# Four edits to a fused attention and mixture-of-experts kernel: opening order, half-size steps for the first pairs, a later request for the second batch, one engine for the last tile

## The chip, the core and the metric

The kernel runs on one core of a Trainium2 chip. The metric is the device time of one execution in microseconds, as the median of three runs. TensorE (PE) does matrix products into PSUM, VectorE (DVE), ScalarE (ACT) and GpSimd (POOL) do the elementwise work, SyncE (SP) issues nearly all DMA transfers, and 16 DMA engines carry them.

## What is computed

```python
scores = np.matmul(z, z.transpose(0, 2, 1)) / S      # 8 batches, S = 3072, z: 64 wide
attn = np.maximum(scores, 0.0) ** 2
x = (u * np.matmul(attn, v)).reshape(B * S, 256)     # u, v: 256 wide
# then a mixture of 8 experts over the rows of x, capacity 768 rows each, top 1:
# row -> expert by argmax(x @ w_gate); rows past the capacity give 0
out[i] = gate[i] * (np.maximum(x[i] @ w1[e], 0) @ w2[e])
```

Experts fill up in the order of the rows. So only the first 14 blocks of 512 rows are computed on the straight path (two batches of six blocks and two blocks of a third), and a guarded loop covers other data.

## The kernel before, in words

**Blocks and pairs.** A block is 512 rows of the output. It sums over 12 pairs; a pair is two tiles of 128 rows of v. For a pair that is made, PE computes scores (`team`, L924), ACT does relu twice and a square (L941, L946), DVE splits the square into a high and a low half-precision part (`hi` L950, `lo` L959), and PE adds up `acc` with three products per tile and 128 rows (L1070): 24 products of 128x256 a pair, half of a run of 48 that the trace shows as 5.41 us. The pairs of a block are p = 0 to 11 for the first, 12 to 23 for the second, 24 to 35 for the third, and so on; the blocks are counted from 0 in the code, block 1 being the second.

**What is not made again.** The scores are symmetric. A block writes the parts that later blocks need to `kept` in memory (`keep`, L981) and later blocks read them back transposed into `ld` (`load`, L897; asked for four pairs ahead, L1039). The part for the very next block goes straight to `nx` (L974), and a corner of the block on the diagonal is turned in the same way (L965). Block 1 writes six of these halves of 512 KB, block 2 four, block 3 two. Block 2 reads the pairs 24 and 25 back, block 3 the pairs 36, 37, 40 and 41, block 4 six pairs, block 5 eight.

**Scaling.** v is split into two half-precision parts too. For this the largest magnitude of a whole batch of v must be known: six parts of 512 KB are loaded (`ld_v`, L363), each reduced by ACT or DVE (`v_abs`, L484 and L73), then `v_red` (L492), a maximum over the partitions on POOL, and three DVE steps (`v_bits`) that make a power of two from it. Only then `v_piece` can split v (ACT L506, DVE L509). z is treated alike (`norm1` to `z_group`); in the first batch its first 12 tiles are turned by PE, the rest by DMA from a second load (`z_again`).

**What sets the order.** Every engine works through its own queue in order. The order is written when the kernel is built: a planner (`weave`, `Chain`) keeps a model clock of each engine and emits the next stage of a chain where it fits. The opening, up to the third pair, is instead written out by hand in `to_scores` and `to_sums`: `go(c, n)` emits the next n steps of a chain, `warm_up(n)` emits n products that nobody reads, which fill PE's queue. A batch that isn't the first is prepared by chains of low rank: a load waits until the model's DMA clock is close to now, and the squares and maxima follow some 20 us later.

**Where the second batch is asked for.** `hook(p)` calls `prepare` when a new block begins: for batch 1 at the start of block 1 (p = 12), for batch 2 at the start of the first block of batch 1. The last step of its z, a swap of halves, is held until pair p + 27.

**The last tile.** In `ffn` the rows of an expert's output are scaled from PSUM in two steps, ACT from one half of the accumulator (L1242) and DVE adding the other (L1248), and scattered by POOL (L84). For the very last tile both parts are summed on PE already, and ACT and DVE scale 128 columns each, into one tile `ys`.

Of the kernel before, what the change touches and what calls it, by code (L numbers as in the profile page):

```python
# [18 lines left out]
P = 128  # L19
# [7 lines left out]
def attention_moe_kernel(ctx: ExitStack, tc: tile.TileContext, u, v, z, w_gate, w1, w2, out, cap):  # L27
# [306 lines left out]
    def prepare(bt, first=False, swap=()):  # L334
# [140 lines left out]
        def v_abs(i):  # L475

            act = first and i in (0, 2, 4, NV)
# [12 lines left out]
        def v_red():  # L490
            bt.vmx = sm.tile([P, 1], F32, tag="vmx", name="vmx")
            nc.vector.tensor_reduce(out=bt.vmx, in_=bt.vm[:, 0:NM], axis=AX.X, op=ALU.max)  # L492
# [5 lines left out]
        def v_bits():  # L498
            bt.vs, bt.vinv = pow2(bt.vma, 1, 14 if first else 12, "vs")
            bt.v2 = sb.tile([P, JT, 2, D], F16, tag="big", name="v2")  # L500

        def v_piece(t0, k):
# [4 lines left out]

            def lo():
# [4 lines left out]

            return [[("ACT", 0.19 + 0.21 * k, hi, None)], [("DVE", 0.06 + 0.285 * k, lo, key("v", t0 // 2) if t0 + k > t0 // 2 * 2 + 1 else None)]]

        def factor():
            q = sm.tile([P, 1], F32, tag="cb0", name="cb0")
            q2 = sm.tile([P, 1], F32, tag="cb1", name="cb1")
            bt.cb = sm.tile([P, 1], F32, tag="cb", name="cb")
# [12 lines left out]
        if first:  # L532
            tz = [(ld_z(i)(), op("SP", 0.75))[1] for i in range(zparts)]
# [50 lines left out]
        def to_scores():  # L584
# [8 lines left out]
            go(A[0])  # L593
            go(G[0], 3)
# [5 lines left out]
            go(A[1])  # L600

        def to_sums(follow, more):
# [4 lines left out]
            go(follow[0])  # L607
# [3 lines left out]
            go(G[2])  # L611
# [13 lines left out]
            for t, k in ((0, 1), (1, 1), (2, 2)):  # L625
# [9 lines left out]
            go(V[2])  # L635
            go(G[2])
# [4 lines left out]
            for i in range(2, JT // 2):  # L641
# [195 lines left out]
    def attention(blocks, hook):  # L837

        NP = len(blocks) * NPAIR
        prs, acc, xs, ut, sct, sq, corner = {}, {}, {}, {}, {}, {}, {}  # L840
# [89 lines left out]
        def follow(p, s, w, t):  # L930
# [29 lines left out]

            def turn(c):
# [17 lines left out]
            def keep():  # L979
# [7 lines left out]
                  [("DVE", 0.07 + w * 0.00107, hi, None, bt.key("vs")), ("DVE", 0.29 + w * 0.0021, lo, (aid, "a", p))]]  # L987
# [46 lines left out]
        for p in range(NP):  # L1034
# [11 lines left out]
            for c in range(cc):  # L1046
                if c % (cc // 2) == 0:
                    scores_to(p + 3 if p > 3 else p + 2 if p or c else 0)
                    weave()
                if c == 0:  # L1050
# [5 lines left out]
                if i == 0 and c % 2 == 0:  # L1056
# [8 lines left out]
                for jj in (0, 1):  # L1065
# [114 lines left out]
    def ffn(wx, sx, n, final):  # L1180
# [43 lines left out]
        for t in range(T):  # L1224
# [14 lines left out]
            def scale(t=t, y=y, end=end):  # L1239
# [4 lines left out]
            def add(t=t, y=y, end=end):  # L1244
                if end:
                    ts(ys[t][:, D // 2:], y[:, 0, D // 2:], g[:, t:t + 1], ALU.mult)
                else:
                    nc.vector.scalar_tensor_tensor(out=ys[t], in0=y[:, 1], scalar=g[:, t:t + 1], in1=ys[t],  # L1248
                                                   op0=ALU.mult, op1=ALU.add)

            Chain([[("ACT", 0.36, scale, None)], [("DVE", 0.4, add, (fid, "y", t))],
# [51 lines left out]
    with tc.manual_schedule():  # L1303
# [40 lines left out]
        def hook(p):  # L1344
# [4 lines left out]
            if g == 0 and ib == (b == 0) and b + 1 in bats:  # L1349
# [82 lines left out]
```

## Time and profile before

| | us |
|---|---|
| median of three runs (782.4 to 784.85) | 783.13 |
| the profiled execution | 783.24 |
| its span in the profile | 781.4 |

The profiled execution took 783.24 us, its span as the profile has it is 781.4 us. Times in a row of the timeline are counted from the start of the span; the first number is the start, the second the time until the last instruction of that row ended. "x2" is two instructions of a kind in a row, and a bracket tells how long the engine sat idle before, and what ended that. SPq is SyncE's queue, which issues DMAs.

### The profile page before, as it was taken

What the parts mean: (1) busy time and instruction counts of PE and PEld (TensorE: products, weight loads), DVE (VectorE), ACT (ScalarE), POOL (GpSimd) and SP (SyncE); (2) the same over time, 40 slices, a digit from 0 to 9 for tenths busy, and PEclk for the clock granted to TensorE, in tenths of its full rate; (3) what the DMA queues carried; (4) which work ended last, traced back from release to release, by engine and by line L of the source; (5) the groups of instructions that cost most, each with busy time, mean ns of one, the idle gap of its engine ahead of it and who ended that gap; (6) DMA issues with size and microseconds to landing.
All of it is one profiled execution on the core that took longest, in us unless ns stands there. A gap on an engine that the chain in (4) does not pass through costs nothing.

```text
span 781.4 us, 16289 instructions
## 1 busy us (share of the span) xinstructions
PE 770.1 (99%) x6476; PEld 569.9 (73%) x6476; DVE 515.4 (66%) x1134; ACT 401.2 (51%) x690; POOL 120.8 (15%) x122
## 2 busy tenths in 40 slices
PE   9999999999999999999999999999999999999996
PEld 3787878888887777878888877886666666656664
DVE  7996888853517789974553258989576575574651
ACT  6966545533206657663431048675455464463541
POOL 0000102020202010210202020202420321313302
PEclk9999999999999999999999999999999999999999
DMA  7659999999978949999979959960698955944001
GB/s 223 147 193 196 250 202 228 207 217 183 182 156 182 289 147 183 236 199 215 204 145 194 171 165 240 320 178 22 216 299 297 321 143 216 294 129 174 28 15 44
DMA packets 283830, 149.49 MB, mean 191 GB/s; under 512 B 229741, under 2 KB 255674, under 8 KB 283744
## 3 DMA queue, kind: packets, MB, share of 16 engines
q1 hardware_dynamic: 278848, 135.57, 71.8%
q0 software_dynamic: 4896, 12.79, 4.7%
q8 instruction: 52, 0.85, 0.5%
q14 instruction: 34, 0.28, 0.1%
HBM read 36.25 MB, written 59.92 MB: 123 GB/s over the span
## 4 chain that ended last, share of the span: by engine, by line
PE 92%; DMA 2%; DVE 2%; SPq 1%; ACT 1%; issue 0%; POOL 0%; POOLq 0%; ACTq 0%
PE acc L1070 52%; PE hps L1211 15%; PE yps L1235 15%; PE sc L924 8%; DMA ld<-kept 1%; SPq L897 1%; DMA wraw<-in_moe_w 1%; PE lg L696 1%; PE warm L151 1%; DMA zraw<-in_z 1%; ACT a L946 0%; DVE wt L1138 0%; ACT r L941 0%; DVE hl L950 0%; DVE zz L425 0%
## 5 line engine op out<-in xcount | busy, mean ns | idle before, releaser
L1070 PE MATMUL acc<-v,hl 128*128 128x256 f16 x2280 | 261.0, 273 | 0.0
L1070 PEld LDWEIGHTS <-hl 128*128 128x128 f16 x2280 | 219.8, 98 | 34.2 <-issue 5.1
L941 ACT ACTIVATE r<-sc 128x512 f32<-128x512 f32 (+1 forms) x212 | 105.6, 550 | 166.2 <-PE sc L924 164.4
L1211 PE MATMUL hps<-fxt,wt 128*128 128x384 f16 (+2 forms) x816 | 127.4, 316 | 0.4 <-DVE hh L1197 0.3
L1235 PE MATMUL yps<-wt,hh 128*128 128x256 f16 (+1 forms) x776 | 126.6, 324 | 0.0
L959 DVE TENSOR_TENSOR hl<-a,hl 128x1024 f16<-128x1024 f32 (+1 forms) x106 | 118.2, 1115 | 3.6
L84 POOL DMA_INDIRECT disp<-xr,slot x54 | 60.8, 1126 | 378.3 <-ACT r L941 139.0
L1211 PEld LDWEIGHTS <-wt 128*128 128x128 f16 x816 | 77.6, 98 | 47.7 <-issue 0.9
L1235 PEld LDWEIGHTS <-hh 128*128 128x128 f16 x776 | 75.7, 98 | 48.5
L1070 PE MATMUL acc<-v,ld 128*128 128x256 f16 x960 | 109.2, 273 | 1.9 <-DMA ld<-kept 1.9
L946 ACT ACTIVATE a<-r 128x1024 f32<-128x1024 f32 (+1 forms) x106 | 102.6, 968 | 2.2
L1070 PEld LDWEIGHTS <-ld 128*128 128x128 f16 x960 | 93.0, 98 | 13.3 <-DMA ld<-kept 2.2
L950 DVE CAST hl<-a 128x1024 f16<-128x1024 f32 (+1 forms) x106 | 67.6, 638 | 49.9 <-ACT a L946 49.1
L1197 DVE SCALAR_TENSOR_TENSOR hh<-hps,hh 128x384 f16<-128x384 f32 (+2 forms) x136 | 70.6, 530 | 34.0 <-ACT hh L1196 33.6
L1196 ACT ACTIVATE hh<-hps 128x384 f16<-128x384 f32 (+2 forms) x136 | 63.7, 472 | 50.4 <-PE hps L1211 49.0
L84 POOL DMA_INDIRECT out<-ys,sid x48 | 53.4, 1112 | 128.4 <-DVE ys L1248 74.6
L924 PE MATMUL sc<-zz 64*128 64x512 f16 (+1 forms) x636 | 71.5, 356 | 0.3 <-DVE zz L425 0.2
L1242 ACT ACTIVATE ys<-yps,sg 128x256 f32<-128x256 f32 (+1 forms) x48 | 22.5, 471 | 72.6 <-PE yps L1235 68.2
L1070 PE MATMUL acc<-v,nx 128*128 128x256 f16 x504 | 58.5, 273 | 0.0
L1248 DVE SCALAR_TENSOR_TENSOR ys<-yps,sg,ys 128x256 f32<-128x256 f32 x47 | 22.6, 482 | 51.3 <-ACT ys L1242 50.8
L1070 PEld LDWEIGHTS <-nx 128*128 128x128 f16 x504 | 48.5, 98 | 8.3 <-issue 2.8
L678 ACT ACTIVATE xr<-x,rsr 128x256 f16<-128x256 f32 x54 | 24.8, 502 | 55.4 <-DVE rsr L60 51.8
(133 smaller groups left out, 484.2 us busy)
## 6 DMA issues: line engine op xcount, KB each, us to landing
out<-zero SPq DMA_DIRECT2D x48, 512.0 KB, 9.6
kept<-hl SPq DMA_DIRECT2D x40, 512.0 KB, 4.8
wraw<-in_moe_w SPq DMA_DIRECT2D x32, 512.0 KB, 6.4
vraw<-in_v SPq DMA_DIRECT2D x18, 512.0 KB, 6.4
u<-in_u SPq DMA_DIRECT2D x13, 512.0 KB, 5.1
zraw<-in_z SPq DMA_DIRECT2D x2, 768.0 KB, 6.3
zz<-zz SPq DMA_DIRECT2D x4, 384.0 KB, 4.5
xt<-xr SPq DMA_TRANSPOSE x54, 2.8
```

Of the source, the lines that this page charges most:

```text
L84: r = nc.gpsimd.indirect_dma_start(out=dst, out_offset=bass.IndirectOffsetOnAxis(ap=idx, axis=0), in_=src, in_offset=None, bounds_check=bo ...
L678: return lambda: nc.scalar.activation(st.x16[:, c, 0:D], st.x[:, c, :], AF.Copy, scale=st.rs[:, c:c + 1])
L924: nc.tensor.matmul(s[jj][:, 0:w], lhsT=bt.zz[rows, (kl + jj) % 2, j * P:(j + 1) * P], rhs=bt.zz[rows, (ql + jj) % 2, q0:q0 + w], start=(i ...
L941: nc.scalar.activation(sct[p][:, jj, :], s[jj][:, 0:w], AF.Relu)
L946: nc.scalar.activation(sq[p], sct.pop(p), AF.Square)
L950: nc.vector.tensor_copy(hl[:, :, :, 0, :], sq[p].rearrange("p j (t k) -> p j t k", k=HB))
L959: nc.vector.tensor_sub(hl[:, :, :, 1, :], a.rearrange("p j (t k) -> p j t k", k=HB), hl[:, :, :, 0, :])
L1070: nc.tensor.matmul(o, lhsT=a(h, jj, c), rhs=bt.v2[:, j, l], start=(i + jj + h + l + c % 2 == 0), stop=(i == NPAIR - 1 and jj + h == 2), sk ...
L1196: Chain([[("ACT", 0.05 + w * 0.00083, lambda: nc.scalar.activation(th, src, AF.Relu), None)], [("DVE", 0.07 + w * 0.00104, lambda: nc.vect ...
L1197: [("DVE", 0.07 + w * 0.00104, lambda: nc.vector.scalar_tensor_tensor(out=tl, in0=src, scalar=0.0, in1=th, op0=ALU.max, op1=ALU.subtract), ...
L1211: nc.tensor.matmul(o, lhsT=wx.w1[:, d, wp, f * P:(f + 1) * P], rhs=sx.xt[:, xp * DC + d, a:a + w], start=(q == 0), stop=(q == len(seq) - 1))
L1235: nc.tensor.matmul(y[:, 0 if end else l], lhsT=hid(i, f)[:, sl], rhs=w[:, l], start=(f + i == 0 and l != 1), stop=(f == FC - 1 and i == 1) ...
```

## The change

- Opening, loads: parts 0 and 1 of z are asked for in one DMA; v's part 0 is asked for from ACT's queue, behind a one-column Square that reads a cell which DVE fills with 2^-112 at the very beginning. That cell takes part in the maximum.
- Opening, order: v's part 1 is reduced by ACT, ahead of z's third group, instead of by DVE. z's `lo` of the third group and half of the first pair's `lo` come before v's maximum is known. `v_bits` makes the factor in two steps instead of three; the inverse moves to `factor`, which runs in the second half of the first block. The warm-up products after the first scores go from 20 to 13.
- First two pairs by tiles: `lo` in two halves of 128x512, v's piece for the second pair's `lo` in two of 128x256, and PE goes through the first tile for all four row groups, then through the second. v's piece for the third pair, and the third pair's `hi` and `lo`, get fixed places.
- The second batch's z and v are asked for at the start of block 2 instead of block 1 (p = 24), and the hold on the swap moves with p, to pair 51.
- The last tile is scaled by ACT alone, all 256 columns.

```diff
@@ prepare
-                    bt.vm = sm.tile([P, NV + 1], F32, tag="vm", name="vm")
+                    bt.vm = sm.tile([P, NV + 2], F32, tag="vm", name="vm")
+                    if first:
+                        nc.vector.memset(bt.vm[:, NM:NM + 1], 2.0 ** -112)
...
-                nc.sync.dma_start(out=zt[:, i * k:(i + 1) * k], in_=zr[:, i * k:(i + 1) * k])
+                o = slice(0, 2 * k) if first and i == 0 else slice(i * k, (i + 1) * k)
+                nc.sync.dma_start(out=zt[:, o], in_=zr[:, o])
...
-                nc.sync.dma_start(out=t, in_=vr[:, 4 * i:4 * i + 4, :])
+                if first and i == 0:
+                    one = sm.tile([P, 1], F32, tag="one", name="one")
+                    nc.scalar.activation(one, bt.vm[:, NM:NM + 1], AF.Square)
+                (nc.scalar if first and i == 0 else nc.sync).dma_start(out=t, in_=vr[:, 4 * i:4 * i + 4, :])
...
-            act = first and i in (0, 2, 4, NV)
+            act = first and i in (0, 1, 2, 4, NV)
...
-            bt.vs, bt.vinv = pow2(bt.vma, 1, 14 if first else 12, "vs")
+            if first:
...
+                ts(e, bt.vma.bitcast(I32), 23, ALU.logical_shift_right)
+                ts(rs, e, -float(1 << 23), ALU.mult, float(268 << 23), ALU.add)
+                bt.vs, bt.vinv = rs.bitcast(F32), inv.bitcast(F32)
+                bt.v_inv = lambda: ts(inv, rs, -1.0, ALU.mult, float(254 << 23), ALU.add)
+            else:
+                bt.vs, bt.vinv = pow2(bt.vma, 1, 12, "vs")
...
+            if first and t0 == 2:
+                return [[("ACT", 0.61, hi, None)], [("DVE", 0.38, lo_one(0), None), ("DVE", 0.38, lo_one(1), key("v", 1))]]
@@ to_scores
             go(A[0])
+            go(A[1])
             go(G[0], 3)
...
-            go(A[1])
@@ to_sums
             go(A[3])
-            go(follow[0])
+            go(G[2])
+            go(follow[0], 2)
             go(A[4])
             warm_up(2)
             third = more()[0]
-            go(G[2])
...
             go(vr, 3)
             go(follow[0])
-            warm_up(11)
+            warm_up(2)
             go(G[2])
-            warm_up(2)
+            warm_up(9)
             more()
-            warm_up(5)
...
             go(follow[1], 2)
             go(V[2])
+            go(follow[1])
+            go(V[2])
...
             go(third)
+            go(V[4])
+            go(third)
+            go(V[4])
+            go(third)
@@ attention, follow
-                  [("DVE", 0.07 + w * 0.00107, hi, None, bt.key("vs")), ("DVE", 0.29 + w * 0.0021, lo, (aid, "a", p))]]
+                  [("DVE", 0.07 + w * 0.00107, hi, None, bt.key("vs")), *([("DVE", 0.29 + w * 0.0021, lo, (aid, "a", p))] if p >= EARLY else
+                    [("DVE", 0.65, lo_half(0), None), ("DVE", 0.65, lo_half(1), (aid, "a", p))])]]
@@ attention, main loop
-            for c in range(cc):
+            for c, jjs in ([(c, (jj,)) for jj in (0, 1) for c in range(cc)] if p < EARLY else [(c, (0, 1)) for c in range(cc)]):
...
-                for jj in (0, 1):
+                for jj in jjs:
@@ ffn, the last tile
-                o = slice(0, D // 2 if end else D)
-                nc.scalar.activation(ys[t][:, o], y[:, 0, o], AF.Copy, scale=g[:, t:t + 1])
+                nc.scalar.activation(ys[t], y[:, 0], AF.Copy, scale=g[:, t:t + 1])
...
-                if end:
-                    ts(ys[t][:, D // 2:], y[:, 0, D // 2:], g[:, t:t + 1], ALU.mult)
@@ hook
-            if g == 0 and ib == (b == 0) and b + 1 in bats:
+            if g == 0 and ib == 2 * (b == 0) and b + 1 in bats:
                 prepare(bats[b + 1], swap=(("pair", p + 2 * NPAIR + 3),))
```

`EARLY` is 2 for the first batch and 0 otherwise.

## Rows read from the trace of the kernel before

**Rows 1.** The page: busy time, share of the span and instructions of each engine.
```profile
PE 770.1 (99%) x6476; PEld 569.9 (73%) x6476; DVE 515.4 (66%) x1134; ACT 401.2 (51%) x690; POOL 120.8 (15%) x122
```

**Rows 2.** Timeline of PE, 94 to 260 us: start, length, what; in brackets idle before.
```profile
102.18 2.79 PE L1070 MATMUL acc<-v,ld 128*128 128x256 f16 x24 [1.91 <-DMA ld<-kept]
...
137.24 5.40 PE L1070 MATMUL acc<-v,ld 128*128 128x256 f16 x48
```

**Rows 3.** Chain of waits, 70 to 106 us: start, length, what.
```profile
93.38 0.58 SPq L363
...
94.00 8.13 DMA ld<-kept
```

**Rows 4.** Windows: stretch, length, busy of each engine, PEclk, DMA share, GB/s.
```profile
80.00:100.00 20.00, 20.00 (x202) 16.39 (x199) 16.53 (x36) 9.12 (x14) 4.88 (x4) 1.00 1.09 254
...
120.00:140.00 20.00, 20.00 (x189) 16.36 (x188) 16.16 (x37) 9.94 (x15) 5.34 (x5) 1.00 1.08 266
```

**Rows 5.** Timeline of SP's queue, 50 to 260 us.
```profile
83.95 0.54 SPq L363 DMA_DIRECT2D vraw<-in_v  x1
...
125.69 8.51 SPq L897 DMA_TRANSPOSE ld<-kept  x2
```

**Rows 6.** DMA issues, 124 to 136 us: count, median us from issue to landing.
```profile
ld<-kept SPq DMA_TRANSPOSE x2, 6.6
```

**Rows 7.** Windows of the opening, columns as in Rows 4.
```profile
4.00:5.00 1.00, 1.00 (x5) 0.46 (x4) 0.54 (x1) 0.82 (x2) 0.00 (x0) 1.00 0.90 254
...
9.00:10.00 1.00, 0.99 (x10) 0.45 (x8) 0.97 (x4) 0.77 (x3) 0.00 (x0) 1.00 1.08 375
```

**Rows 8.** Timeline of the opening, up to the common factor of v.
```profile
3.80 0.63 ACT L370 ACTIVATE sq<-zraw 128x512 f32<-128x512 f32 x1 [1.77 <-DMA zraw<-in_z]
...
5.80 0.63 ACT L370 ACTIVATE sq<-zraw 128x512 f32<-128x512 f32 x1 [0.56 <-DMA zraw<-in_z]
...
8.22 1.06 ACT L484 ACTIVATE junk<-vraw 128x1024 f32<-128x1024 f32 x1 [1.79 <-DMA vraw<-in_v]
...
11.18 1.06 ACT L484 ACTIVATE junk<-vraw 128x1024 f32<-128x1024 f32 x1 [0.42 <-DMA vraw<-in_v]
...
12.19 2.32 DVE L73 TENSOR_REDUCE vm<-vraw 128x1 f32<-128x1024 f32 x2
...
15.81 0.63 ACT L484 ACTIVATE junk<-vraw 128x512 f32<-128x512 f32 x1 [0.38 <-DMA vraw<-in_v]
...
15.81 0.69 DVE L73 TENSOR_REDUCE vm<-vraw 128x1 f32<-128x512 f32 x1 [0.16 <-DMA vraw<-in_v]
...
17.64 0.15 DVE L60 TENSOR_SCALAR vsr<-vsi 128x1 int32<-128x1 int32 x1
```

**Rows 9.** Timeline of the opening, after the common factor of v.
```profile
17.71 1.22 DVE L959 TENSOR_TENSOR hl<-a,hl 128x1024 f16<-128x1024 f32 x1
...
18.64 1.04 ACT L946 ACTIVATE a<-r 128x1024 f32<-128x1024 f32 x1
...
18.84 0.87 DVE L509 SCALAR_TENSOR_TENSOR v<-vraw,vsr,v 128x256 f16<-128x256 f32 x2
...
21.58 0.75 DVE L509 SCALAR_TENSOR_TENSOR v<-vraw,vsr,v 128x512 f16<-128x512 f32 x1
...
25.18 1.22 DVE L959 TENSOR_TENSOR hl<-a,hl 128x1024 f16<-128x1024 f32 x1
...
26.39 5.41 PE L1070 MATMUL acc<-v,hl 128*128 128x256 f16 x48
```

**Rows 10.** Timeline, 36 to 60 us, a difference of half the usual width.
```profile
55.44 0.69 DVE L959 TENSOR_TENSOR hl<-a,hl 128x512 f16<-128x512 f32 x1
```

**Rows 11.** Timeline of the last tile and the one before it.
```profile
771.42 0.48 ACT L1242 ACTIVATE ys<-yps,sg 128x256 f32<-128x256 f32 x1 [2.13 <-PE yps L1235]
...
774.04 0.37 ACT L1242 ACTIVATE ys<-yps,sg 128x128 f32<-128x128 f32 x1 [2.14 <-PE yps L1235]
...
774.44 0.35 DVE L58 TENSOR_SCALAR ys<-yps,sg 128x128 f32<-128x128 f32 x1 [2.03 <-ACT ys L1242]
```

More of the change, by code (lines that the diff above doesn't have):

```diff
@@ L491, in v_red @@
             bt.vmx = sm.tile([P, 1], F32, tag="vmx", name="vmx")
-            nc.vector.tensor_reduce(out=bt.vmx, in_=bt.vm[:, 0:NM], axis=AX.X, op=ALU.max)
+            nc.vector.tensor_reduce(out=bt.vmx, in_=bt.vm[:, 0:NM + first], axis=AX.X, op=ALU.max)
         def v_all():
@@ L498, in v_bits @@
         def v_bits():
-            bt.vs, bt.vinv = pow2(bt.vma, 1, 14 if first else 12, "vs")
+            if first:
+                e = sm.tile([P, 1], I32, tag="vse", name="vse")
+                inv = sm.tile([P, 1], I32, tag="vsi", name="vsi")
+                rs = sm.tile([P, 1], I32, tag="vsr", name="vsr")
+                ts(e, bt.vma.bitcast(I32), 23, ALU.logical_shift_right)
[4 more added lines that the diff above has]
+                bt.vs, bt.vinv = pow2(bt.vma, 1, 12, "vs")
             bt.v2 = sb.tile([P, JT, 2, D], F16, tag="big", name="v2")
@@ L506, in hi, with lo_one, f @@
                 nc.scalar.activation(bt.v2[:, o, 0, :], bt.vraw[i][:, a:a + k], AF.Copy, scale=bt.vs)
+            def lo_one(j):
+                def f():
+                    nc.vector.scalar_tensor_tensor(out=bt.v2[:, t0 + j, 1, :], in0=bt.vraw[i][:, a + j], scalar=bt.vs,
+                                                   in1=bt.v2[:, t0 + j, 0, :], op0=ALU.mult, op1=ALU.subtract)
+                return f
             def lo():
@@ L518, in factor @@
             q2 = sm.tile([P, 1], F32, tag="cb1", name="cb1")
+            if first:
+                bt.v_inv()
             bt.cb = sm.tile([P, 1], F32, tag="cb", name="cb")
@@ L532, in prepare @@
         if first:
-            tz = [(ld_z(i)(), op("SP", 0.75))[1] for i in range(zparts)]
+            tz = [0.0] * zparts
+            for i in (0, 2):
+                ld_z(i)()
+                tz[i] = op("SP", 0.75 if i else 1.5)
+            tz[1] = tz[0]
             clk["DMA"] += 1.9
@@ L640, in to_sums @@
             go(third)
-            for i in range(2, JT // 2):
+            go(V[4])
+            go(third)
+            go(V[4])
+            go(third)
+            for i in range(3, JT // 2):
                 Chain(v_piece(2 * i, 2), -2, done[key("vs")], gate=("pair", i - 2 + (2 < i < 6)))
@@ L839, in attention @@
         NP = len(blocks) * NPAIR
+        EARLY = 2 if hasattr(blocks[0][0], "to_scores") else 0
         prs, acc, xs, ut, sct, sq, corner = {}, {}, {}, {}, {}, {}, {}
@@ L959, in lo, with lo_half, f @@
                 nc.vector.tensor_sub(hl[:, :, :, 1, :], a.rearrange("p j (t k) -> p j t k", k=HB), hl[:, :, :, 0, :])
+            def lo_half(j):
+                def f():
+                    a, hl = sq[p]
+                    nc.vector.tensor_sub(hl[:, j, :, 1, :], a[:, j].rearrange("p (t k) -> p t k", k=HB), hl[:, j, :, 0, :])
+                return f
             def turn(c):
@@ L1055, in attention @@
                     a = prs.pop(p)
-                if i == 0 and c % 2 == 0:
+                if i == 0 and c % 2 == 0 and 0 in jjs:
                     k = bank[0] - 3
@@ L1238, in ffn, with scale, add @@
                 weave()
-            def scale(t=t, y=y, end=end):
+            def scale(t=t, y=y):
                 ys[t] = sb.tile([P, D], F32, tag="hl", name="ys", bufs=5)
-                o = slice(0, D // 2 if end else D)
-                nc.scalar.activation(ys[t][:, o], y[:, 0, o], AF.Copy, scale=g[:, t:t + 1])
-            def add(t=t, y=y, end=end):
-                if end:
-                    ts(ys[t][:, D // 2:], y[:, 0, D // 2:], g[:, t:t + 1], ALU.mult)
[L1247 to L1251, printed above, removed]
+                nc.scalar.activation(ys[t], y[:, 0], AF.Copy, scale=g[:, t:t + 1])
+            def add(t=t, y=y):
+                nc.vector.scalar_tensor_tensor(out=ys[t], in0=y[:, 1], scalar=g[:, t:t + 1], in1=ys[t],
+                                               op0=ALU.mult, op1=ALU.add)
+            Chain([[("ACT", 0.36, scale, (fid, "y", t) if end else None)],
+                   [] if end else [("DVE", 0.4, add, (fid, "y", t))],
                    [("POOL", 1.04, lambda t=t: scatter("out", out, tid[:, t:t + 1], ys[t], NTOK - 1), None)]],
```

6 lines of the change are left out of this document (3 added, 3 removed).

## The prediction

> **What bounds the kernel now.** I read the page first: PE is busy for 770.1 us [rows 1], so out of the execution's 783.24 us only 13.1 are left that are not products, and a faster engine elsewhere is worth nothing unless it takes away PE idle time, or products that nobody reads. I then looked for PE's gaps, stage by stage. There are three places: the opening, where PE is kept busy with warm-up products until v is scaled; one gap in the middle; and the end, after the last product. The rest is products back to back, so what is gained in one place stays gained, unless a new gap opens behind it.
>
> The gap in the middle stands on PE's timeline: 1.91 us before the second read-back of block 2 (pair 25) [rows 2]. SP's queue and the chain of waits say why: one part of batch 1's v was issued at 83.95, ahead of the first read-back [rows 5], another at 93.38 between the two, and the second read-back took 8.13 us to land, at 102.13 [rows 3]. PE wanted it at 102.18 - 1.91 = 100.27. The windows show the DMA engines full there (share 1.09, 254 GB/s) [rows 4].
>
> For the opening I followed the timeline back from the first real products. Two places decide. The factor of v is ready at 17.64 + 0.15 = 17.79, and before it both engines wait for v's last part: ACT 0.38 us, DVE 0.16, both starting at 15.81 [rows 8]. Behind it DVE works without a gap until the low part of the third pair ends at 25.18 + 1.22 = 26.40, and PE begins that pair at 26.39 [rows 9]. Its third product is the first to read that low part; 48 products take 5.41 us, so it starts about 0.22 later, at 26.61. There are 0.2 us to spare, no more. An earlier first product alone therefore wins nothing: PE would wait at the third pair. What counts is when the factor is ready, and how long DVE's list behind it is.
>
> **The change, part by part.**
>
> *The later request.* Batch 1's z and six parts of v leave block 1. So the two parts of v no longer stand ahead of the late read-back; each is 0.52 MB, 2.1 us at 254 GB/s [rows 4], and two make 4.1. Without them it lands near 98.0, 2.3 us before PE wants it. So the gap closes: -1.91. The gain can't exceed the gap, and is 0 if something else of that stretch is as late.
>
> The same loads now lie in block 2, so the next thing to be late would be block 3's read-backs (pairs 36, 37). Before, the two were issued from 125.69 on, 8.51 us for both [rows 5], so the second at about 129.9; they land 6.6 us after issue [rows 6], the second at 136.5. (The row is a median of the two, so this is an estimate.) PE wants it half of its run after 137.24 [rows 2], at 139.9. That is 3.4 us of room, and the whole front moves alike. What comes in front of them, by the picture of block 1, is two parts of v: at 266 GB/s [rows 4] 2 x 1.97 = 3.9 us. What goes: block 2 writes two halves of 0.52 MB fewer than block 1, but that is in the 3.4 already; z's four transposes, which now fall in block 3, leave. So the sum is 3.4 - 3.9, about -0.5 at worst and some 2 of room at best. I take no new gap, and keep 0.5 for the range. ACT's and DVE's steps for batch 1 move along and have time until block 6; that cover goes only if their loads slip by blocks.
>
> *Loads of the opening.* DMA moved 254 GB/s between 4 and 5 us and 375 between 9 and 10 [rows 7]. If a second queue fills that hole, v's last part comes 1 x (375 - 254) / 375 = 0.3 us earlier. z in one DMA less frees SP's queue a step earlier, which is the same gain seen from SP. On ACT, the small Square and the issue stand ahead of the first square of z, where ACT waits 1.77 us for z anyway [rows 8]: no cost, unless issuing takes longer than that. The fill on DVE stands ahead of the constants, under the same wait for z. The inverse goes to DVE in the second half of block 0, one step of 0.15, and the swap held to pair 51 is wanted in block 6 only: nothing for both.
>
> Here the trace and a rule part. The trace has all these loads in one queue, and its rate between 4 and 5 us is a third below that of 9 to 10 [rows 7]. The Trainium skill, in "DMA: Bandwidth & Descriptors", section "Issuing engines are not separate DMA queues", says that DMAs of all issuers run on the same 16 engines and interleave, so that a second issuer saves only the time to issue. By that rule the 0.3 would be nothing; the second rival gives what the interleaving would do to z.
>
> *Order before the factor.* DVE loses one of the two maxima that took 2.32 us [rows 8] and gains half of the first pair's low part, 0.69 [rows 10]: 0.47 less. It was free 0.16 before 15.81 [rows 8], so it is free near 15.2, or 15.5 if z comes 0.3 later. ACT gets the maximum: 1.06. From v's first part at 8.22 to 15.43 ACT was waiting only for v's third part (0.42) and a little for PE [rows 8]. Its list from v's first part on is then 7.21 - 0.42 + 1.06 = 7.85. If that part still lands at 8.22 ACT reaches v's last part at 16.07, 0.26 late. Behind z it took 8.22 - 5.80 = 2.42 us [rows 8], where 0.52 MB at 375 GB/s [rows 7] take 1.4; from a queue of its own it may land up to 1.0 earlier, and I take 0.6, giving 15.5. So all three, the load, DVE and ACT, say 15.5 to within 0.3: the last maxima start 0.3 earlier than 15.81 (bounds: 0.26 later, 0.6 earlier). The factor then takes one DVE step less, 0.15 [rows 8]. Factor: 0.3 + 0.15 = 0.45 earlier, at 17.34.
>
> *Order behind the factor.* The first pair's low part is now 0.69 instead of 1.22 [rows 9, 10], but the saving is lost: the second pair's `hi` must wait for ACT's square, which ended at 18.64 + 1.04 = 19.68, and ACT's list from the factor to there is unchanged. Then come the halves: two of 0.69 for one of 1.22 (+0.16), and two pieces of one tile, which together took 0.87, for one of 0.75 (+0.12) [rows 9]. So the third pair's low part ends at 26.40 - 0.45 + 0.28 = 26.23. With the 0.2 to spare, PE starts the third pair 0.37 us earlier than before. The 7 warm-up products fewer keep PE out of the way; they are in this number, not beside it. Bounds: 0.2 us slower (factor 0.11 later, DVE's list 0.28 longer, 0.2 to spare) and 0.9 faster (last part 0.6 and step 0.15 earlier, the 0.2 to spare, with the cost of the halves hidden in DVE's waits for ACT).
>
> *The last tile.* DVE began its half only when ACT had ended, and ended at 774.44 + 0.35 = 774.79; ACT alone, at 0.48 for 256 columns, ends at 774.04 + 0.48 = 774.52 [rows 11]. The scatter starts on the one that is last: -0.27. Bounds: 0 and -0.35.
>
> *Sum.* -1.91 - 0.37 - 0.27 = -2.55, from 783.24 to 780.69. The median of the runs is 0.11 below that execution, so 780.6.
>
> **The rivals.**
>
> *The gap comes back a block later.* For it: block 2's DMA was as full as block 1's (1.08 and 1.09) [rows 4], and the room at pair 37 is about the size of what comes in. If three transfers of 1.97 stand in front of the read-back, it is 5.9 - 3.4 = 2.5 us late. 780.6 + 2.5 = 783.1: no difference. Against it: block 2 has two writes fewer, and the planner holds v back when its own DMA clock is busy.
>
> *The opening gives nothing, or less.* If v's first part takes half the engines while z's last third is under way (0.26 MB at 254 GB/s, 1.0 us), z lands up to 1.0 later than the 5.80 of before [rows 8]. DVE is then free for v's last part at 15.2 + 1.0 = 16.2, 0.4 late; less the step of 0.15, with the longer list (0.28) and less the 0.2 to spare that is 0.3 slower instead of 0.37 faster. 780.6 + 0.7 = 781.3: no difference that can be told, though the gap in the middle is gone. This is also the case in which the part of the change that gives its name to the opening doesn't do what it says. The rule of the Trainium skill named above is this rival's reason; in the opening of this trace only SP issues loads, so nothing shows it here.
>
> *Slower: block 3's read-backs stand behind all of v.* One mechanism: SP's queue is in order, and if the planner places all six parts of v before pair 37's read-back they cost 6 x 1.97 = 11.8 us of transfers, less 3.4 of room: PE stands 8.4 us. 780.6 + 8.4 = 789.0. It turns slower by over 0.3% from 5 us of standing on, which is more than four parts of v in front. Against it: in block 1 the parts were spread over the whole block, one of them was still issued between two read-backs [rows 3].
>
> **How the numbers follow.** 0.3% is 2.35 us, about what a measurement of this kernel can tell from no change; the border of faster is 780.78, close to my sum, so the forecast's own spread lies on both sides. Chances: the forecast 0.52, of which 0.45 below the border; the gap a block later 0.25; the opening giving nothing 0.13; slower 0.10. That makes faster 0.45, same 0.07 + 0.25 + 0.13 = 0.45, slower 0.10. Range: the low end is the forecast with the opening's best (0.5 more), the last tile's best (0.1) and half a microsecond of spread between runs, 779.5; the high end is the gap coming back, 783.1, with a little of that spread, 783.4. The slower case and half of the spread beyond the gap stay outside.
>
> **What would show it.** The gap before pair 25 gone from PE's idle time, and no read-back of pairs 36, 37, 40, 48 in front of a new one. The factor of v ready near 17.3, and PE's third pair starting near 26.0, with z's last square starting no later than 6.1. ACT alone on the last tile, the scatter 0.3 us sooner after the last product. I am wrong if PE's second block starts less than 0.2 us earlier, if ACT reaches v's last part later than it lands, or if a read-back in blocks 3 to 5 is waited for.

## The result and the profile after

The changed kernel took 787.34 us (median of 7 runs), beside 782.40 for the kernel before in the same comparison: a ratio of 1.0068, 95% interval 1.0048 to 1.0088. By the ratio it is 5.3 us slower, where 2.55 less were forecast, and it lies outside the range. The profiled execution took 789.47 us, its span 787.7.

PE's line of the page (columns as in [rows 1]) shows where to look. PE is busy for 771.6 us, 1.5 more than before although it makes seven products fewer, and idle for 787.7 - 771.6 = 16.1 us, 4.8 more than before. DVE and ACT did about the same work as before, so the loss is not in their busy sums.

```profile
PE 771.6 (98%) x6469; PEld 569.7 (72%) x6469; DVE 514.1 (65%) x1136; ACT 401.8 (51%) x693; POOL 121.8 (15%) x122
```

PE's timeline of the changed kernel, blocks 2 to 5 (start, length, what; idle before in brackets), shows where it stood:

```profile
100.02 5.40 PE L1112 MATMUL acc<-v,ld 128*128 128x256 f16 x48
...
137.69 5.40 PE L1112 MATMUL acc<-v,ld 128*128 128x256 f16 x48
...
155.59 2.25 PE L1112 MATMUL acc<-v,hl 128*128 128x256 f16 x19 [0.29 <-DVE hl L994]
...
177.01 4.09 PE L1112 MATMUL acc<-v,ld 128*128 128x256 f16 x36 [1.21 <-DVE x L1054]
...
211.79 5.42 PE L1112 MATMUL acc<-v,ld 128*128 128x256 f16 x48 [1.27 <-DMA ld<-kept]
...
232.38 5.42 PE L1112 MATMUL acc<-v,ld 128*128 128x256 f16 x48 [1.68 <-DMA ld<-kept]
```

The first two rows are the places that the prediction watched. The gap of 1.91 us before pair 25 is gone: pairs 24 and 25 now run their 48 products without a break, and so do pairs 36 and 37, as they did before [rows 2]. But four gaps are new, 0.29 + 1.21 + 1.27 + 1.68 = 4.45 us, and the first two of them end on DVE, not on a DMA.

The other loss is in the opening. Its timeline in the changed kernel, and the last of these rows as the kernel before has it:

```profile
0.74 1.28 ACT L368 ACT_TABLE_LOAD   x1 [0.74 <-PEq L1459]
0.91 0.42 ACTq L369 DMA_DIRECT2D vraw<-in_v  x1
...
2.04 0.20 ACT L368 ACTIVATE one<-vm 128x1 f32<-128x1 f32 x1
7.05 1.67 ACT L376 ACTIVATE sq<-zraw 128x512 f32<-128x512 f32 x3 [4.81 <-DMA zraw<-in_z]
...
11.80 0.62 PE L425 MATMUL ztp<-ident,zhl 128*128 128x128 f16 x8 [1.56 <-DVE zhl L414]
13.45 2.93 PE L959 MATMUL sc<-zz 64*128 64x512 f16 x12
...
20.12 0.15 DVE L60 TENSOR_SCALAR vsr<-vse 128x1 int32<-128x1 int32 x1
...
28.65 5.68 PE L1112 MATMUL acc<-v,hl 128*128 128x256 f16 x48
34.26 1.47 PE L959 MATMUL sc<-zz 64*128 64x512 f16 x12
```

```profile
31.73 1.47 PE L924 MATMUL sc<-zz 64*128 64x512 f16 x12
```

The second row is the surprise. The code puts the one-column Square (2.04) in front of the issue of v's part 0, but the issue went out at 0.91, during the table load: it depends on nothing that the Square writes. z's squares then begin at 7.05, where they ran at 3.80 and 5.80 before [rows 8]; PE gets z 1.56 us too late, the factor of v ends at 20.27 instead of 17.79, and the third pair starts at 28.65 instead of 26.39 [rows 9]. The scores after it begin at 34.26 instead of 31.73, 2.53 later.

The windows of the same stretch (columns as in [rows 4]), and the first of them in the kernel before:

```profile
3.00:4.00 1.00, 1.00 (x3) 0.30 (x2) 0.48 (x3) 0.00 (x0) 0.00 (x0) 1.00 0.90 176
4.00:5.00 1.00, 1.00 (x4) 0.40 (x3) 0.00 (x0) 0.00 (x0) 0.00 (x0) 1.00 1.10 371
...
14.00:16.00 2.00, 2.00 (x12) 0.57 (x6) 2.00 (x4) 1.25 (x4) 0.00 (x0) 0.50 1.28 245
```

```profile
3.00:4.00 1.00, 1.00 (x3) 0.29 (x2) 0.45 (x3) 0.20 (x1) 0.00 (x0) 1.00 1.04 301
```

Between 4 and 5 us the DMA engines moved 371 GB/s instead of 254 [rows 7], but between 3 and 4 only 176 instead of 301, so over the two they moved no more than before (547 for 555). The hole was not filled, it moved, and part of what came were bytes of v that nobody could use yet, while ACT and DVE did nothing at all between 4 and 5. The last row of the changed kernel shows a granted clock of 0.50, the 1.2 GHz level: 12 products for scores take 2.93 us there and 1.47 at 34.26, and the difference is about what PE is busy longer than before.

The last tile came out as forecast. The changed kernel's timeline, and the scatter of the kernel before:

```profile
780.04 0.47 ACT L1283 ACTIVATE ys<-yps,sg 128x256 f32<-128x256 f32 x1 [2.15 <-PE yps L1277]
780.79 0.97 POOL L84 DMA_INDIRECT out<-ys,sid  x1 [1.13 <-ACT ys L1283]
```

```profile
775.07 0.97 POOL L84 DMA_INDIRECT out<-ys,sid  x1 [1.41 <-DVE ys L58]
```

The scatter starts 0.75 after ACT does; before it was 1.03 (ACT's start is in [rows 11]). That is 0.28 less, where 0.27 was forecast.

Summed up: 2.53 (opening) + 4.45 (new gaps) - 1.91 (old gap) - 0.28 (last tile) = 4.8. The two profiled executions are 6.2 apart and the medians 5.3 or so by the ratio. The rest is spread over three places, as the same rows of the two profiles show. The changed kernel is 2.53 late behind the opening, 0.45 at the sum of block 2 (136.58 for 136.13) and 5.57 at that of block 5 (247.20 for 241.63), which is 0.5 more than the gaps alone explain; it is still 5.57 late at the last block (528.08 for 522.51). The mixture adds 0.43 (last tile 780.04 for 774.04). And from the start of the last scatter to the end of the span it is 6.9 us instead of 6.3; that tail is 5.5 to 6.9 in all the profiles of this case, old kernel or new.

### The profile page after: what moved, and what is told of

Its sections match the earlier page's. It is cut to its first block, busy times and chain, and to the rows that moved or that the text cites. A ratio compares the mean times of both kernels' runs of the same rounds, so it can differ in the third digit from the quotient of the medians.

```text
span 787.7 us, 16284 instructions
## 1 busy us (share of the span) xinstructions
PE 771.6 (98%) x6469; PEld 569.7 (72%) x6469; DVE 514.1 (65%) x1136; ACT 401.8 (51%) x693; POOL 121.8 (15%) x122
## 4 chain that ended last, share of the span: by engine, by line
PE 81%; issue 7%; DMA 4%; DVE 4%; ACT 1%; POOL 1%; SPq 1%; POOLq 0%; ACTq 0%
PE acc L1112 46%; PE hps L1253 13%; PE yps L1277 13%; PE sc L959 8%; DMA ld<-kept 2%; DMA fxt<-disp 2%; POOL out L84 1%; DMA zraw<-in_z 1%; DVE v L530 1%; SPq L723 1%; PE lg L730 1%; DVE hl L985 0%; SPq L932 0%; DVE hl L994 0%; DVE wt L1180 0%
## 5 line engine op out<-in xcount | busy, mean ns | idle before, releaser
L994 DVE TENSOR_TENSOR hl<-a,hl 128x1024 f16<-128x1024 f32 (+1 forms) x104 | 115.7, 1113 | 3.5
L1283 ACT ACTIVATE ys<-yps,sg 128x256 f32<-128x256 f32 x48 | 22.6, 472 | 72.6 <-PE yps L1277 68.2
```

Of the source, the lines that this page charges most:

```text
L994: nc.vector.tensor_sub(hl[:, :, :, 1, :], a.rearrange("p j (t k) -> p j t k", k=HB), hl[:, :, :, 0, :])
```

## Where the new gaps come from

The views of SP's queue, ACT and DVE in block 3 of the changed kernel, in order of time:

```profile
126.00 9.19 SPq L932 DMA_TRANSPOSE ld<-kept  x2
...
136.43 3.73 SPq L1006 DMA_TRANSPOSE corner<-hl  x2
140.25 4.22 SPq L932 DMA_TRANSPOSE ld<-kept  x2
144.56 3.07 SPq L466 DMA_TRANSPOSE zz<-zhl  x2
...
149.02 0.61 ACT L459 ACTIVATE zhl<-zraw,zb 128x384 f16<-128x384 f32 x1 [6.33 <-DMA zz<-zhl]
...
149.67 0.62 DVE L462 SCALAR_TENSOR_TENSOR zhl<-zraw,zb,zhl 128x384 f16<-128x384 f32 x1 [4.11 <-ACT zhl L459]
150.21 3.46 DVE L73 TENSOR_REDUCE vm<-vraw 128x1 f32<-128x1024 f32 x3
...
159.44 0.15 DVE L60 TENSOR_SCALAR vsr<-vsi 128x1 int32<-128x1 int32 x1
...
176.26 1.29 DVE L1054 TENSOR_TENSOR x<-acc,u 128x512 f32<-128x512 f32 x2
...
204.37 6.88 SPq L932 DMA_TRANSPOSE ld<-kept  x2
```

The kernel before has these two rows for the fourth group and for the factor of v:

```profile
116.16 0.62 ACT L453 ACTIVATE zhl<-zraw,zb 128x384 f16<-128x384 f32 x1
...
135.25 0.15 DVE L60 TENSOR_SCALAR vsr<-vsi 128x1 int32<-128x1 int32 x1
```

Read it as one chain. The second batch's z is made in four groups, but there are only three tiles `zhl`: the fourth has to wait until the first has been transposed. In the kernel before that preparation fell into block 2, where the four groups ran on ACT at 109.41, 111.98, 113.43 and 116.16 and the first transposes were issued at 110.71. A block later SP's queue is at that moment working off block 3's four read-backs (126.00 and 140.25) and the corner, and the transposes come at 144.56, behind all of them. ACT works in order, so it stands 6.33 us at the fourth group, and with it everything behind: DVE has no new squares to split, stands 4.11, and has four maxima of v still before it. The factor of v is ready at 159.59, where it was 135.40 in the kernel before. (That alone is not late: the batch is asked for 35.5 us later, at 98.73 instead of 63.22. What counts is what then falls together.) From 160.81 to 182.61 DVE's list then holds v's pieces between the splits that PE is waiting for, the routing of the rows, and the sum of the block: `x` is formed at 176.26, and PE stands 1.21 for it. SP's later steps slip too: a pair of read-backs is issued at 204.37 that was issued at 195.88 before.

## The experiments

The kernel before ran beside every experiment, on the same chip: 788.96 us in the first comparison (the first four), 789.51 in the second (only v later, the tile of its own, the order alone and v behind the read-back), 782.39 in the third, and 782.70 in the last, the second run of the order alone. Times of different comparisons are not set against each other, ratios are. All eight profiles of the first two comparisons, which are from two chips, have one gap of 3.6 to 4.1 us in the mixture stage (557 to 564 us) that no other profile has, so it belongs to no edit. Of the kernel before there is no profile from these two chips; where a row of theirs is set against one of before, that is across chips.

**The later request alone.** The kernel before with one line changed.

```diff
-            if g == 0 and ib == (b == 0) and b + 1 in bats:
+            if g == 0 and ib == 2 * (b == 0) and b + 1 in bats:
```

> The kernel before with the later request of batch 1 and nothing else. Theory: the later request by itself closes the gap of 1.91 us before pair 25 and opens the new ones of blocks 3 to 5 (0.29, 1.21, 1.27 and 1.68 us, 4.45 in all in the changed kernel), so about 2.5 us slower than before, 785, with PE idle inside 160 to 240 us. Rival: the new gaps come from the opening, whose other lengths let the planner order everything behind it in another way; then the gap of 1.91 closes and nothing opens, 780.5. PE's third pair stays at 26.4 in both.

Measured: 792.59 us, ratio 1.0045 [1.0028, 1.0063], 3.6 us slower. PE's gaps in the profile of this kernel, and ACT's stand:

```profile
154.06 2.25 PE L1070 MATMUL acc<-v,hl 128*128 128x256 f16 x19 [0.54 <-DVE hl L959]
...
175.51 4.09 PE L1070 MATMUL acc<-v,ld 128*128 128x256 f16 x36 [1.23 <-DVE x L1012]
...
211.34 5.42 PE L1070 MATMUL acc<-v,ld 128*128 128x256 f16 x48 [2.32 <-DMA ld<-kept]
...
231.17 5.41 PE L1070 MATMUL acc<-v,ld 128*128 128x256 f16 x48 [0.92 <-DMA ld<-kept]
...
147.50 0.61 ACT L453 ACTIVATE zhl<-zraw,zb 128x384 f16<-128x384 f32 x1 [6.58 <-DMA zz<-zhl]
```

Gaps in the same four places, 5.0 us in sum, with the opening of before: they belong to the later request. It closes the old gap and opens more than it closes.

**The request back.** The changed kernel with that line undone.

```diff
-            if g == 0 and ib == 2 * (b == 0) and b + 1 in bats:
+            if g == 0 and ib == (b == 0) and b + 1 in bats:
```

> The changed kernel with batch 1 asked for in block 1 again. Theory of the later request: the 4.45 us of gaps in blocks 3 to 5 go, a gap near 1.9 before pair 25 comes back, and what is left over before is the late opening (third pair 2.26 us late), so about 784.5 to 785. Rival, that the gaps follow from the opening: they stay, and the time is 787 or more. The third pair stays near 28.6 in both.

Measured: 791.07 us, 1.0032 [1.0018, 1.0047]. The gaps of blocks 3 to 5 are gone, one of 1.26 before pair 25 is there again, z's squares begin at 6.81 and the scores after the third pair at 34.16. So the opening alone costs PE 2.4 us against the profile of before, 1.7 against that of the experiment just above, which has the opening of before on the same chip (scores at 32.49), and this kernel is slower by 2.5.

**v's part 0 from SP's queue.** The rest of the change stays.

```diff
-                (nc.scalar if first and i == 0 else nc.sync).dma_start(out=t, in_=vr[:, 4 * i:4 * i + 4, :])
+                nc.sync.dma_start(out=t, in_=vr[:, 4 * i:4 * i + 4, :])
```

> The changed kernel with v's part 0 asked for from SP's queue, behind z. Theory of the shared engines: part 0 was issued at 0.91, before the small Square that was to hold it (2.04), and took half the engines from z; without that z's squares end near 6.5 instead of 8.7, TensorE doesn't idle 1.56 us in front of z's turning and keeps its higher clock, the third pair starts by 26.4, 2.3 us or more sooner than in the changed kernel; about 785. Rival, that asking for two parts of z in one DMA is what makes z late: the first square still starts near 7, and nothing is won.

Measured: 790.53 us, 1.0027 [1.0013, 1.0041]. ACT and PE in the opening of this kernel:

```profile
5.09 1.67 ACT L376 ACTIVATE sq<-zraw 128x512 f32<-128x512 f32 x3 [2.85 <-DMA zraw<-in_z]
...
25.99 5.68 PE L1112 MATMUL acc<-v,hl 128*128 128x256 f16 x48
31.60 1.47 PE L959 MATMUL sc<-zz 64*128 64x512 f16 x12
```

z is back in time, the granted clock is 1.00 from 12 to 16 us, and the third pair begins at 25.99, as forecast (26.02). But look at its length: 5.68 us instead of 5.41 [rows 9]. PE starts it early and then waits inside it for the low part, so the next scores come at 31.60 where they were at 31.73: against that one profile the order of the opening gains 0.13. One profile is too few here. The five that have the opening of before (before twice, the later request alone, only v later, and the tile of its own) put these scores at 31.73 to 32.49, median 32.08; the five with the new order and v from SP's queue put them at 31.57 to 31.98, median 31.61. By the medians the order gains 0.5; pairs from one chip give 0.1 to 0.9. The two largest gaps in blocks 3 to 5 are 0.90 and 0.97. With the old gap gone (0.66 to 1.91, see the second profile of before below), at least 0.13 in the opening and the last tile's 0.28, the rows explain at most 0.8 of the measured 2.1; the rest I did not find.

**v's part 0 held until the Square has run.** In the changed kernel the Square writes a cell of the tile that the DMA fills, so that the DMA must wait for it.

```diff
-                    one = sm.tile([P, 1], F32, tag="one", name="one")
-                    nc.scalar.activation(one, bt.vm[:, NM:NM + 1], AF.Square)
+                    nc.scalar.activation(t[:, 0, 0:1], bt.vm[:, NM:NM + 1], AF.Square)
```

> The changed kernel with a real hold: the small Square writes into the tile of v's part 0, so that ACT's DMA has to wait for it. Theory of the shared engines: the DMA is issued behind 2.2 us, its first bytes come when half of z is in, z's squares end at about 7, and the opening wins 1.5 to 2 us over the changed kernel: about 785.5. Rival, that ACT's queue as such or the maximum that ACT got is the cause: z's squares end near 7 but the factor of v is still ready at 20, and the time stays at 787.

Measured: 792.50 us, 1.0051 [1.0033, 1.0069]. The opening of this kernel:

```profile
2.27 0.49 ACTq L368 DMA_DIRECT2D vraw<-in_v  x1
5.21 1.67 ACT L375 ACTIVATE sq<-zraw 128x512 f32<-128x512 f32 x3 [2.98 <-DMA zraw<-in_z]
10.16 1.06 ACT L489 ACTIVATE junk<-vraw 128x1024 f32<-128x1024 f32 x1 [3.27 <-DMA vraw<-in_v]
...
13.41 1.47 PE L958 MATMUL sc<-zz 64*128 64x512 f16 x12 [1.89 <-ACT zz L430]
```

The first two rows confirm the mechanism: issued at 2.27 instead of 0.91, the DMA leaves z alone (5.21). The next two show a price I had not seen: v's parts 0 and 1 now land late, their maxima stand on ACT at 10.16 and 11.21 ahead of the copy of z, and PE waits 1.89 for that copy. The scores after the third pair begin at 33.56, so of the 1.5 to 2 us that the opening was to win over the changed kernel, 0.7 came (33.56 for 34.26). Neither moment for ACT's queue is good; SP's order (all of z, then v) is.

**Only v a block later.** The kernel before with z asked for in block 1 and v in block 2.

```diff
-        if not first:
+        def ask_z():
...
+        def ask_v():
...
+            if g == 0 and n == 2:
+                bats[1].ask()
```

> The kernel before; batch 1's z is asked for in block 1 as before, only its v in block 2. With both later (the first run) the time was 1.0045 of before, with 5.0 us of gaps in blocks 3 to 5. Theory: ACT stood 6.6 us in block 3 for a free tile for z's fourth group (its transposes queued on SP behind the read-backs), DVE starved behind it, and v's maxima and splitting then fell together; with z early that stand is gone, the maxima come sooner, and no gap over 0.5 us is left in blocks 3 to 5 and none before pair 25: 0.997 to 0.998 of before. Rival: v's steps on DVE in blocks 3 and 4 are themselves what is too much; the gaps stay, 1.003 to 1.005.

Measured: 791.40 us, 1.0029 [1.0016, 1.0041]. My expectation failed: I had thought that z in its old place would spare ACT the stand. ACT and PE in block 2 of this kernel:

```profile
111.74 0.62 ACT L453 ACTIVATE zhl<-zraw,zb 128x384 f16<-128x384 f32 x1 [6.62 <-DMA zz<-zhl]
...
112.89 1.29 PE L933 MATMUL sc<-zz 64*128 64x512 f16 x6 [0.29 <-ACT r L950]
115.10 1.71 PE L933 MATMUL sc<-zz 64*128 64x512 f16 x6 [0.91 <-ACT r L950]
```

z's groups now begin at 102.70 instead of 109.41, and the fourth again comes to ACT before SP's transposes have freed a tile. The stand is the same, 6.62, and hits PE by way of ACT's relu; between 116 and 120 us the mean granted clock is 0.59. It is not the block that does harm, but the fourth group waiting for a tile.

**The later request with a tile of its own for the fourth group.** The kernel before with the later request and this:

```diff
-                st.zhl = sb.tile([P, ZW, 2, DQ], F16, tag="zhl", name="zhl", bufs=3)
+                own = straight[0] and bt.b == 1 and t0 == 3 * ZW
+                st.zhl = sb.tile([P, ZW, 2, DQ], F16, tag="u" if own else "zhl", name="zhl", bufs=1 if own else 3)
```

> The kernel of the first run (both z and v later, opening of before), but z's fourth group gets a tile of its own (in the place of u, which is idle then), so that ACT needn't wait for z's first transpose. Theory of the stand on ACT: the 6.6 us before the fourth group go, DVE isn't starved, v's factor comes some 5 us earlier (near 153 instead of 158), and the gaps before pairs 36 to 61 shrink to under 1 us in all: 0.998 to 0.999 of before. Rival: it is DVE's amount of work, or SP's queue as such; the gaps stay near 5 us and the time at 1.0045.

Measured: 789.84 us, 1.0005 [0.9994, 1.0017]. The fourth group on ACT, and the one gap that is left:

```profile
140.55 0.60 ACT L454 ACTIVATE zhl<-zraw,zb 128x384 f16<-128x384 f32 x1
...
226.74 5.42 PE L1071 MATMUL acc<-v,ld 128*128 128x256 f16 x48 [1.08 <-DMA ld<-kept]
```

ACT no longer stands for the fourth group, the factor is ready 4.7 us earlier (153.34 for 158.07), and of PE's idle time between 20 and 260 us, 5.1 us in the kernel with the later request alone, 1.2 is left. One tile removes nearly all of the loss, though the 0.998 to 0.999 that was expected did not come. Both gaps that ended on DVE are gone. One gap of 1.08 at 226.74, before a read-back, remains; what makes that read-back late is not shown.

**The order of the opening and the last tile alone.** The changed kernel with v's part 0 from SP's queue and the request back (both diffs above).

> The changed kernel with two things undone: v's part 0 from SP's queue behind z, and batch 1 asked for in block 1. What is left is the order of the opening, the halves, the two-step factor and the last tile. Theory: the third pair starts 0.3 to 0.4 us earlier, the last tile gives 0.27, the gap before pair 25 is back at 1.3 to 1.9: 0.999 of before, no difference that can be told. Rival: the new order in the opening moves the planner so that other gaps come: 1.002 or more.

Measured: 788.37 us, 0.9982 [0.9970, 0.9995]. As its gain is small, it was run once more, on another chip:

> The changed kernel with v's part 0 in SP's queue and the request back in block 1, once more and likely on another chip. Theory (the order of the opening gives 0.4 us and the last tile 0.3, everything else is as before): third pair near 26.0 to 26.3, ratio 0.998 to 0.9995. Rival (the 0.9982 measured first was the spread of one chip): 0.9995 to 1.001.

Measured: 782.11 us, 0.9985 [0.9971, 0.9999]. Both times faster than the kernel before, by 1.2 to 1.4 us, though not by the 0.3% set as the bound; by its ratio it beats both kernels. Of that, 0.28 is the last tile, and the opening is 0.1 (scores after the third pair at 31.61 and 31.67, for 31.73) or, by the medians above, 0.5; the rest is not shown by any one row. The gap before pair 25 is 0.93 in the first of the two profiles, and in the second there is none.

**v behind the read-back.** The last kernel, with three parts of batch 1's v held back until the second read-back of block 2 has been asked for.

```diff
-                Chain([[("SP", 1.46, ld_v(i), None)], [mark(i)]], 2, slow=20.0)
+                Chain([[("SP", 1.46, ld_v(i), None)], [mark(i)]], 2, slow=20.0,
+                      gate=("pair", 22) if straight[0] and bt.b == 1 and i >= 3 else None)
```

> The one before, and in block 1 the parts 3 to 5 of batch 1's v are held until pair 22, that is until the read-backs of pairs 24 and 25 have been issued. Theory: the gap before pair 25 (1.3 to 1.9 us) is made by these parts standing in front of the read-back; it closes, v's factor comes a few us later in block 2 and 3 without harm, and the kernel beats both: 0.996 to 0.997 of before. Rival: the read-back is as late without them (writes and transposes alone fill the engines), the gap stays and the time is that of the one before; or v's later steps open a gap in block 3.

Measured: 788.56 us, 0.9990 [0.9980, 1.0001]. PE has no gap left between 20 and 260 us, its span is 1.2 us shorter than that of the kernel it comes from (786.3 for 787.5), and yet the two can't be told apart in time: the gap closed as expected, the 0.996 to 0.997 did not come. Closing the gap before pair 25 is worth less than the profile of one execution made it.

**The kernel before, profiled again,** unchanged.

> The kernel before, unchanged, for a profile from the chip of the other kernels and for the spread that a comparison of one kernel with itself leaves. Both theories: 1.000, interval within 0.002; third pair at 26.4, the gap of 1.9 us before pair 25 there, PE busy for about 238.1 of the 240 us between 20 and 260.

Measured: 781.99 us, 0.9999 [0.9985, 1.0012]. The same place as in [rows 2], in this second profile of the same kernel:

```profile
101.27 2.79 PE L1070 MATMUL acc<-v,ld 128*128 128x256 f16 x24 [0.66 <-DMA ld<-kept]
```

0.66 us, not 1.91. I had expected 1.9. The gap is a race between a transfer and PE, and its size differs between executions, or between chips: the three profiles above of kernels that ask for the whole batch in block 1 and hold nothing back (the request back, and the order alone twice) have 1.26, 0.93 and none. The opening differs too, with the third pair at 26.73 instead of 26.39.

**v's part 0 from ACT's queue alone,** in the kernel before.

```diff
-                nc.sync.dma_start(out=t, in_=vr[:, 4 * i:4 * i + 4, :])
+                (nc.scalar if first and i == 0 else nc.sync).dma_start(out=t, in_=vr[:, 4 * i:4 * i + 4, :])
```

> The kernel before with one edit, v's part 0 from ACT's queue. Theory (that DMA goes out at about 0.9 and takes half of the engines from z): z's squares begin at about 7 instead of 3.8 to 5.8, PE's turning of z 2 us later, granted clock down to 0.5 for some us before the third pair, third pair 2 to 2.6 us later than 26.4, ratio 1.002 to 1.004. Rival (the order of the opening costs it, not the queue; v0 early frees ACT): z's squares less than 0.5 later, third pair within 0.5 of 26.4, ratio 0.999 to 1.001.

Measured: 783.15 us, 1.0013 [1.0002, 1.0025]. ACT's and PE's rows of this kernel:

```profile
0.74 0.48 ACTq L363 DMA_DIRECT2D vraw<-in_v  x1
...
5.46 0.63 ACT L370 ACTIVATE sq<-zraw 128x512 f32<-128x512 f32 x1 [2.92 <-DMA zraw<-in_z]
...
8.01 0.63 ACT L370 ACTIVATE sq<-zraw 128x512 f32<-128x512 f32 x1 [0.24 <-DMA zraw<-in_z]
...
28.51 5.41 PE L1070 MATMUL acc<-v,hl 128*128 128x256 f16 x48
```

The queue alone makes z 2 us late and the third pair 1.8 (28.51, for 26.73 in the profile of before from the same chip). Only 1.0 of it reaches the end, less than the 1.002 to 1.004 expected. There is no gap before pair 25 in this kernel: PE comes later, and the read-back is there. 1.8 - 0.66 = 1.1. The clock stayed at 1.00 from 10 to 20 us, so the drop that the changed kernel has is not made by this DMA alone.

**The changed kernel mended:** v's part 0 from SP, the fourth group's own tile, the later request kept.

> The changed kernel with v's part 0 back in SP's queue and a tile of its own for the second batch's fourth group of z. Theory (the later request costs what ACT's stand at that tile costs, the opening what ACT's queue costs; the rest of the change gains): third pair near 26.0, no gap before pair 25, ACT not standing for the fourth group, gaps in blocks 3 to 5 of 1.2 us together at most, last tile 0.28 shorter; ratio 0.997 to 0.998, at least as fast as the version with the request back (0.9982). Rival (v later is late for reasons beside that tile): gaps of 2 us or more at the read-backs of blocks 4 and 5, ratio 0.9985 to 1.000.

Measured: 781.70 us, 0.9994 [0.9984, 1.0004]: no difference, where 0.997 to 0.998 was expected. Its rows:

```profile
26.37 5.68 PE L1113 MATMUL acc<-v,hl 128*128 128x256 f16 x48
...
228.02 2.79 PE L1113 MATMUL acc<-v,ld 128*128 128x256 f16 x24 [0.26 <-DMA ld<-kept]
```

Both mends do what they should: one gap of 0.26 is all that is left in blocks 2 to 5. But against the profile of before from the same chip there is little to win: 0.66 - 0.26 of gap, 0.09 in the opening (scores after the third pair at 31.98 for 32.07) and 0.28 at the last tile, 0.8 in all, of which 0.5 shows. In the mixture stage this profile has two gaps, 0.22 and 0.56 (530.14 and 570.16), that the other has not.

## Why the prediction was wrong

**The later request, right half.** The gap before pair 25 closed, for the reason given, and the read-backs of pairs 36 and 37 were not late; the rival that let the gap come back a block later, and the slower one with all of v in front of pair 37, did not happen. The size was an upper one: -1.91 was the gap in one execution, a second profile of the same kernel has 0.66.

**The later request, the step that failed:** "ACT's and DVE's steps for batch 1 move along and have time until block 6; that cover goes only if their loads slip by blocks." There was time until block 6 for the values, but not for the engines' queues. I followed v's loads past SP and left out the four transposes of z on the same queue except as something that "leaves", and did not ask who waits for them: ACT, in order, because the fourth group needs the first one's tile. The kernel with the later request alone has the loss (1.0045), a tile of its own for that group takes nearly all of it away (1.0005), and where z stayed and v moved, the stand went with z's groups. That shows the cause of the loss and of the gaps that end on DVE. The gaps before the read-backs of blocks 4 and 5 are less sure: their sum is 0.2 to 3.2 us in the four profiles that have the stand and the later request, and 0.3 and 1.1 in the two with the tile of its own.

**Loads of the opening.** Taken at -0.3, in fact about +2. I let z be at most 1.0 late, for "if v's first part takes half the engines while z's last third is under way". The false step is the moment: I took the Square in front of the issue for something that holds it back, so that part 0 would come when most of z had landed. It went out at 0.91, before the Square, and shared the engines with nearly all of z: z's last square began at 7.05 + 1.67 - 0.63 = 8.09 instead of 5.80, 2.3 late, over twice my bound for that rival. The rule of the Trainium skill that the rival named ("DMA: Bandwidth & Descriptors", "Issuing engines are not separate DMA queues": DMAs of all issuers run on the same 16 engines and interleave) agrees with these rows. The gain failed as well: the rate rose in the hole (254 to 371 GB/s) and fell by about as much just before it (301 to 176). And no gain from z in one DMA less shows: with v's part 0 back on SP's queue z's last square began at 5.09 + 1.67 - 0.63 = 6.13, where the two profiles of before have 5.80 and 5.96.

**Order before the factor.** With v's part 0 back on SP, the factor ended at 17.60, 0.19 earlier than in the profile of before, where 0.45 was forecast. Over the same ten profiles as above it is 17.79 to 18.54 with the old opening (median 18.12) and 17.59 to 17.99 with the new order (median 17.61), 0.5 earlier. So the size may well be right, but not for the reason given for 0.3 of it: in these kernels there is no second queue that could bring v's last part sooner. How the 0.5 divides between the maxima and the step saved is not shown.

**Order behind the factor.** Right. DVE's list is 0.28 longer, as worked out: 26.40 - 0.19 + 0.28 = 26.49, and the third pair's low part ended at 25.21 + 1.21 = 26.42 in the kernel with the order alone. The third pair's start, 25.99, is early, but PE then waits inside the run. From the factor to the next scores it is 31.61 - 17.61 = 14.00, and 31.73 - 17.79 = 13.94 before: 0.06 more, where the 0.28 less the 0.2 to spare made 0.08.

**The last tile.** Right: 0.28 for 0.27.

The sum by what was measured is 2.5 + 4.45 - 1.91 (or 0.66) - 0.28, between 4.8 and 6.0; the comparison gives 5.3. The slower end had 0.10, for a mechanism that was not the one.

## What to carry to other kernels

When a preparation is moved to another place, follow each queue that it uses there, and above all the tiles that it shares with itself: a step that waits for a buffer on an in-order engine holds back everything behind it, however far off the deadline of its own value is. Don't count on an instruction in front of a DMA's issue to hold it back: here the DMA went out at 0.91 ahead of an instruction at 2.04 that it didn't depend on, and at 2.27 once it did. If a transfer must not compete, give it a dependence, or leave it in the queue whose order is the one wanted. And a gap that ends on a transfer, or a gain of a few tenths, is worth what it is over several executions, not in the one that was profiled.

## What was not expected of the hardware

A DMA issue in ACT's program was seen at 0.74 and 0.91 us, before or beside the table load, and ahead of an ACTIVATE that stands before it in the program (2.04). In the changed kernel the granted clock fell to 0.50 (the 1.2 GHz level) between 14 and 16 us, after PE had stood 1.56 and 0.30 waiting for z, and so it did with the request back, after 1.51 and 0.30; with v's part 0 alone from ACT's queue PE stood 1.23, 0.30 and 0.23 there, and with it held back 0.25, 0.30 and 1.89, and both times the clock stayed at 1.00. What decides between the two stays open.
